# A new hand-written order of the pieces, and four masks placed elsewhere, in a fused threshold-attention and maxout-FFN kernel

## The chip, the core and the metric

The kernel runs on one core of a Trainium2 chip. The metric is the time of one execution in microseconds (us), measured on the device; for a group of runs it is the median. A profile is taken of one execution, and its span goes from the first to the last instruction. The engines are TensorE (PE; its weight loads, PEld, are shown apart), VectorE (DVE), ScalarE (ACT), GpSimd (POOL) and SyncE (SP), which here only issues transfers.

## What is computed

Attention with a threshold: of each row of scaled scores only those within tau = 0.02 of the row's maximum take part in the softmax. Its output, all heads side by side, goes through a maxout network.

```python
# q, k, v: (8, 8, 576, 64) float32; w1, w2, w3: (512, 768); w_out: (768, 512)
scores = scale * np.matmul(q, k.transpose(0, 1, 3, 2))
thresh = np.max(scores, axis=-1, keepdims=True) - tau
scores = np.where(scores >= thresh, scores, -1000000000.0)
scores = scores - np.max(scores, axis=-1, keepdims=True)
attn = np.exp(scores)
attn = attn / (np.sum(attn, axis=-1, keepdims=True) + 1e-09)
attn_out = np.matmul(attn, v)
x = attn_out.transpose(0, 2, 1, 3).reshape(B * S, H * D)      # (4608, 512)
h = np.maximum(np.maximum(x @ w1, x @ w2), x @ w3)
out = h @ w_out
```

## The kernel before

The work is cut into 16 quads (8 batches of two groups of four heads). A quad has 9 chunks of score rows and each chunk two tiles of 128 x 576, so there are 144 chunks and 288 tiles. The last batch is done in two parts of its rows. All scores, transposes, hidden layers, outputs and products pass through four two-bank slots of PSUM, numbered 0 to 3 and called banks below.

A score tile goes like this. PE computes it into a bank (tile `sc`, float32, from `qt`, its half-swapped copy `qs`, and `kt`). DVE takes the row's maximum (`maximum`, line 315). ACT forms what the threshold needs (`exponents`, line 327). Then comes a last pass with the row's sum (`numerators`, line 335). There are two variants, and the string `MASKED` (line 24) chooses one for each tile, with "1" for masked, in the order of the chunks, two digits to a chunk:

- not masked: DVE only reads the bank for the maximum, ACT reads the bank (`exponents`), and ACT makes the last pass as well (`numerators`);
- masked: DVE copies the negated scores to SBUF (tile `z`) together with the maximum, which sets the bank free; ACT works on `z`, and DVE makes the last pass.

Then DVE takes the reciprocals of the chunk's two sums (`reciprocals`, line 341), POOL multiplies both tiles into bfloat16 probabilities `P` (`normalized`, line 345, six buffers), and SP issues a DMA transpose of them into `ptq` (`turned`, line 355). `z` has four buffers for each of the two tiles of a chunk. When a quad's (or part's) chunks are transposed, PE multiplies by `v` (`product`, line 361, tile `o`), DVE and ACT move the result to `xt`, and the FFN (`ffn`, line 434) can run on it: 18 hidden pieces for a batch (tile `ph`; for each block of 128 hidden columns w1, w2 and w3), of which ACT evacuates the first and DVE takes the maximum with the other two, and output pieces (tile `po`), which ACT evacuates and SP stores.

What sets the order is one string, `ORDER` (line 40), read from left to right (lines 718 to 725). Each letter issues one piece (`issue`, line 602), and every engine's instructions are chained in the order in which they are issued (`_Ordered`, line 82). An engine therefore does its own letters in the order of the string; against the other engines it only waits for data and buffers. A digit after S, T, O or F is the bank.

| letter | engine | piece |
|---|---|---|
| S | PE | one score tile |
| T | PE | transposes of q or k for the next quad (tile `tp`) |
| O, N | PE | product of probabilities and v; its ninth rows, for two at once |
| F, B | PE | first and second half of a hidden or output piece |
| m, k | DVE | maximum of a tile; last pass of a masked tile |
| e, n | ACT | exponents of a tile; last pass of a tile that isn't masked |
| r, p, t | DVE, POOL, SP | reciprocals; probabilities (one tile); DMA transpose of a chunk |
| a, c, q | ACT, DVE, POOL | evacuation of transposed q, of transposed k; half-swapped copies `qs` |
| h, v, u | ACT, DVE, ACT | evacuation of the first hidden piece, of the two others, of an output |
| x, w | ACT, DVE | evacuation of a product to `xt` |
| l, y | SP, POOL | loads for a later quad; casts of v |
| g, z | SP, POOL | load of a piece of the weights; its cast to bfloat16 (12 of each) |
| o | SP | store of an output |

"Place" below is the position of a letter (with its digit) in the string, from 0; the string has 2,742. Tiles are numbered from 0 by their digit in `MASKED`. Before the string starts, `beginning` (line 672) transposes the first quad and computes two score tiles.

Of the kernel before, what the change touches and what calls it, by code (L numbers as in the profile page):

```python
# [39 lines left out]
ORDER = """  # L40
mmlS2eS3mmleS1mkllnyT0eS3nS2T1alglermpceS0emT1S3knmaqrpkS1elmqpS2rmeS0ypllneS3mnplleT1mretnnmkS2mcgltlzpqS3e
S0lrpmpeS1etkznenqprnlmpS2S3pmmrmeepS0mnpS2egrpkmpntelS1epmT0kaeerltS3S2tlT0ynmemkeS1nrmpS3ctS2ernnppttT0mlm
pneaS1rtmS3S2pemeS3pqemkmpgneS0rkS1T2qpmqltempyrecpnpS0mqpklS3nemenenS2T1lrpklmerpzapS0pmtryptS3meS2kmeS1S0O
3nnmeempO2NS1eknxrwS0nmeS2rptpqpT3ntmmrnS0tpecmS1pS3eS0tptrmT2S1mmppeatqngleO2ekkleO0rNS3mwxF0elkT2mcnnzpBrp
hS1S2emS0zlpgtpF3F1qemmettkeBqvBS2rnnzF0T3mtBvpnhpkS2meraeF1S0BS3mgevmF2nprS1mepypqBpnF0S3lvkBegF2F1BmhrvS0z
tneBpplzF3nnS2mvBeS1T0mrtT2mhS3pncgpgaS2F0mtBererlmpekvS1emF3S2nntS0pBlemeS1ppzqtS2mvmrF3qentT0pBF1rcmS0pppz
nhenBS3mvO2rmgO1NekglentexnS0F3S1klwmmrnF2plpqypeeBzpBvS0hS1tmF3S2mBtrF1pzpneemrS0vBlneS3mvnS2mrppyS0mnemF1k
S2eS3mreptnepBepmS0F3kpmrS2uutS1kenmnT0arBpekS2emtupueS0mkptpqqO1lltO3emNrlelpkwS2tllxltrlS0F3myF1lmBnpeekph
T2cBF0T3T2vnanqpBS1cvqmF3S2BmneF0hrS1pyperBkF3S2mnBrvmvF0enS1BtS2plmmloppeS3hS0eS1emmtpmF3eekF2BBleF0tlT1vnt
rBvT3aT2haS1pS0kF2crtS3nmBnpmtmF0eS1tqpeeqvBptlmrppF2nveS3lntBmrlF0hS1kpyeBS2mpnvmrenpqyplS3O1qtO0mrNepexkT2  # L50
nS3wF0cS1mrBpmnenS2S1oF3vF0pBtmmeS1pekhlS2toF3rBmmeptynevlT1aBprS2vS0nmmeF1ukketepF3kS1mT2T0rrcBS1ptpqnnaoup
umS0eppmrS2S3mmeeeS0F1eS2qnkpkmT3BS0rnceunrmkmueppS3tlltemO2epO1NotllltS0krwpxS3ppqyF2qnpnmS1BmeS3hF0emmeeF2
BnS1BkrvmnrF3loS0BvpleyyrS2mnpmpphS1ppF0etmS3emllBeF1nF2BtevkrpS0BvS3nS1hmmtleS2lmmetF3tkF0eBpleT1BvrvanT2nF
3cS1BnmF0S2BrhkF3mpeT1vnrBpprveaS0S2nmT1S3pqpncmpS0meeeqmeS1tO2pqmtotlloeO3ltqNF0S1klwBxrpkppS2mrhmF3S0epBmF
2nenS1pvBF0mF3nleBBtottvkS2hF0keF1rurvpmT3BeapkppyrpvS1S2mnS3S0pnemF1mtS3emkS2rpBenepltS0memkmrutpuS2neS3emF
1rmpqkynpS2pqeBemS0uuS2O3kmemekO1NeS0rwT2xoF1olppnT3mnT0BcS2aS3rncqhF0qtF1pBtemmpBkevrF2eS3vlmpnBptnlS0S1S3h
ermmempS2F0ypmF1BBelrteoevnF3T2F0akkqvBBS2nhkymF1pqpnF3verBBS0rvtpmhnS2S1F3mrmlpBpeS0evlmS2eF1pnS3BmnleF2mtl
lvrlttS0eppptyBmS1ehF3lepT2BmltnS0lnltcS1rkvO2O3tmNpmeprT1nnexrapkwS0pqF3qyemT1T2cpBF0S1anepkBS2hvF3S0mreBF1
mekmrnvF2qBeS3vS0unpS2tS1omlrmeppqptlmmnF3pktT0BpecS1eekryuT2uaS0mnS3lomtmrtleF2enpS1kpS3qppnemmS0Bmkerppeue
qS1S0mnurO3kmO1NkwxT0S2eeS1cmpmF3F0kkeBBhF2eF3pvrBS1nnBvpttS0hmemS2mrppF1rpS3BeenmeF0S2vBF1nkvmS3mlnBS0otolh  # L60
F2llterlmF1kBlpypvpBtvteeprS3F0rT2BpS1nnrmpmaS2mtpheS0S3emnF2eT1T0amecBS3ttoS0evyymmS1ppeO2mpqneO3NenqxF0kkt
F1wBT2lolrlklBpS3vphS0cmnF1mtlteS2nqrtBmrpF0vrpqpF3lekBeBpnhF1S2vmT0tlpBS3lS2avmpF0tF1mBrnelekS3evutppmrS2qp
pS1nS0nmF3mrmS1peekenpS2BemmeS0rkS1emuS2tlT0ueT3mcknrannpepF1S0mS3qppBmtotlmlttkrrpeueS0qqmS3lO2ueemoeO0oppt
pkklNwS1lS3xF2mS0BnemehF1kT3mrcnpBS0F2rvS3BltlpnmF1nepmeveS0pkmBS2httnF3eF1mBrBekF0nS2vrBprvpypppS3nmhemeS1S
0F3pF2mmBeBrT1eS0kvnapS3vF1nS2mnBrmmreS3F0pheS1meeBqpnS2mvmeypS1tpS3etlO0qO2mNpmT3neytF1xtlkkrtnweS2ppT0cram
BF3S0BnehvppmeS1rF2qqmT3BF0ncveT3ktnBF2vS1mrnarBhppS0lF3T2qppeBmcS0S1ovmF2mneT3naepBvS0S3enF2mkmrkqpqueenF1n
S2tmS0T3cpqBeupurrS3mmottoS2pS0mttneelotpmS1O3mkkO0rNwrpeexpneF2nkpS0S3S1mBemS0euuppmF1erkS3tltlBptmrF2S0lht
pmeyppBeS1mvO0O3NenmxpS2S1kF0mxemrS3kBF1enF2vBermF0tBhpyppyektBvS1pmF3F2vBkS1BF0nmehS3vrBmtpO2eotpnevO1NkF0S
3krmnrpxpxBhF2S1eBF0mS3F1BnvpmBrS2vS3S0ehemmF1kppmnF2rBvkBF3F0BF1ehBtkvevoF3pptkttO2O0NuprBwS3xS0vmmpeS2ekF1
S3pmF0oeBmrBokettF2peuokoruoF3uhF1pkkF2hvvruF3pF1F2hppF0pvvF3F1vvF2F0F3hvtovhtF1F2F0F3htvF1voF2O0uvO3NvF1xwF  # L70
2hF3F0vF2vhF3F0F2hvF3vvF0F2F3vF0hF2hovF3vF0F2vhF3vvF0vBuuF2BuouoF3uooo
"""


# [684 lines left out]
```

## Time and profile before

| | |
|---|---|
| median of 3 runs | 444.01 us (443.42 to 445.07) |
| the profiled execution | 443.89 us |
| its span | 442.1 us |
| PE busy | 421.6 us (95%) |
| PE weight loads | 306.2 us (69%) |
| DVE busy | 401.2 us (91%) |
| ACT busy | 388.1 us (88%) |
| POOL busy | 320.7 us (73%) |
| granted TensorE clock, mean | 0.988 |

Rows of groups read: line, engine, operation, output from input with shapes, count; busy time and mean length of one in ns; idle time of the engine just before them and what ended most of it. Nearly all instructions carry line 91, the line of the helper that issues them, so the tiles' names tell them apart. Matmuls overlap, and their ends are modelled, so a busy PE isn't PE at its peak. A piece of the chain of waits reads: start, length, engine, tile, line, count.

### The profile page before, as it was taken

The page shows a single profiled execution, that of the slowest core. Times are in us where ns is not written, and L with a number is a line of the kernel's source. Part 1 is how long each engine was busy: PE and PEld are TensorE (multiplying, and loading weights), DVE is VectorE, ACT ScalarE, POOL GpSimd, SP SyncE. Part 2 cuts the span into 40 slices and gives each one's busy share as a digit, 9 for nine tenths or more (in the row PEclk, how much of TensorE's full clock was granted, in tenths as well). Part 3 has the DMA queues.
Part 4 walks back from the last instruction along what each step waited for, and adds up shares of the span by engine and source line. Part 5 has one row for each costly group of instructions (what it writes and reads, how often), then busy time and mean ns, then how long its engine had stood idle before and what let it go on. Part 6 is the DMA issues. An engine that isn't in the chain of part 4 may idle for free.

```text
span 442.1 us, 14065 instructions
## 1 busy us (share of the span) xinstructions
PE 421.6 (95%) x5193; PEld 306.2 (69%) x5193; DVE 401.2 (91%) x1105; ACT 388.1 (88%) x786; POOL 320.7 (73%) x406
## 2 busy tenths in 40 slices
PE   7777799999999999999999999999999999999995
PEld 6443456767778776867687767867677777777762
DVE  2989999999999999999999999999999999999641
ACT  4998999999999999998999999999999999875422
POOL 3898999899976868586777886677769767554500
PEclk9988899999999999999999999999999999999999
DMA  8999989999999998999999999999999978586602
GB/s 234 301 251 204 243 156 223 284 219 213 224 228 177 241 237 169 202 173 283 178 221 188 242 182 222 166 222 193 236 188 177 247 125 165 100 162 137 176 13 108
DMA packets 212773, 87.44 MB, mean 198 GB/s; under 512 B 185824, under 2 KB 199648, under 8 KB 212704
## 3 DMA queue, kind: packets, MB, share of 16 engines
q1 hardware_dynamic: 212000, 85.69, 95.4%
q8 instruction: 41, 0.67, 0.6%
q10 hardware_dynamic: 704, 0.85, 0.6%
q14 instruction: 28, 0.23, 0.2%
HBM read 34.60 MB, written 9.44 MB: 100 GB/s over the span
## 4 chain that ended last, share of the span: by engine, by line
PE 72%; DVE 6%; ACT 4%; POOL 2%; issue 2%; DMA 1%; SPq 0%; POOLq 0%; DVEq 0%
PE ph L91 29%; PE sc L91 25%; PE po L91 9%; PE o L91 6%; ACT z L91 4%; PE tp L91 3%; DVE z L91 2%; DVE unused L91 2%; POOL P L91 1%; POOL qs L91 1%; DVE kt L91 1%; DMA out_dram<-ob 1%; POOL vb L91 0%; DVE xt L91 0%; DVE hT L91 0%
## 5 line engine op out<-in xcount | busy, mean ns | idle before, releaser
L91 POOL TENSOR_SCALAR P<-z,rs 128x576 bf16<-128x576 f32 x288 | 236.2, 834 | 75.2 <-DVE rs L91 21.8
L91 PE MATMUL sc<-kt,qt 64*128 64x320 f32 (+2 forms) x640 | 183.5, 431 | 4.7 <-ACT z L91 2.6
L91 PE MATMUL sc<-kt,qs 64*128 64x256 f32 (+2 forms) x640 | 181.6, 420 | 4.2 <-ACT z L91 2.1
L91 PE MATMUL ph<-xt,w 64*128 64x288 bf16 (+2 forms) x2160 | 170.7, 283 | 0.4 <-DVE xt L91 0.2
L91 PEld LDWEIGHTS <-w 64*128 64x128 bf16 (+1 forms) x2160 | 125.3, 94 | 33.6 <-issue 6.5
L91 DVE TENSOR_SCALAR_CACHE_REDUCE unused<-sc 128x576 bf16<-128x576 f32 x174 | 128.1, 749 | 4.6 <-PE sc L91 3.6
L91 ACT ACTIVATE z<-sc,nm 128x576 f32<-128x576 f32 x174 | 125.3, 740 | 5.3 <-DVE unused L91 2.9
L91 ACT ACTIVATE z<-z 128x576 f32<-128x576 f32 x174 | 117.7, 681 | 0.2
L91 PEld LDWEIGHTS sc<-kt,qs 64*128 64x128 f32 (+1 forms) x640 | 92.2, 179 | 24.3 <-ACT z L91 4.7
L91 PEld LDWEIGHTS sc<-kt,qt 64*128 64x128 f32 (+1 forms) x640 | 91.9, 179 | 19.4 <-ACT z L91 6.2
L91 DVE SCALAR_TENSOR_TENSOR z<-z 128x576 f32<-128x576 f32 x114 | 95.2, 845 | 0.3
L91 ACT ACTIVATE z<-z,nm 128x576 f32<-128x576 f32 x114 | 86.8, 773 | 4.8 <-DVE z L91 4.5
L91 DVE TENSOR_SCALAR_CACHE_REDUCE z<-sc 128x576 f32<-128x576 f32 x114 | 84.7, 751 | 6.9 <-PE sc L91 3.4
L91 POOL COPY qs<-qt 64x640 f32<-64x640 f32 (+3 forms) x68 | 50.2, 738 | 17.8 <-ACT qt L91 14.1
L91 PE MATMUL po<-wo,hT 64*128 64x512 bf16 (+1 forms) x480 | 53.8, 357 | 0.1
L91 ACT ACTIVATE hm<-ph 128x576 bf16<-128x576 f32 (+2 forms) x54 | 32.2, 595 | 20.7 <-PE ph L91 19.8
L91 DVE TENSOR_TENSOR hm<-ph,hm 128x576 bf16<-128x576 f32 (+2 forms) x54 | 37.0, 684 | 8.8 <-PE ph L91 8.7
L91 PEld LDWEIGHTS <-hT 64*128 64x128 bf16 (+1 forms) x480 | 27.5, 97 | 19.0 <-issue 3.8
L91 DVE TENSOR_TENSOR hT<-ph,hm 128x576 bf16<-128x576 f32 (+2 forms) x54 | 37.2, 688 | 2.6 <-PE ph L91 0.5
L91 PE MATMUL o<-ptq,vb 128*64 128x64 bf16 (+2 forms) x544 | 35.3, 281 | 0.1
L91 ACT ACTIVATION_READ_ACCUMULATOR z<-z 128x1 f32 x174 | 34.5, 198 | 0.0
L91 PEld LDWEIGHTS <-vb 128*64 128x64 bf16 x544 | 21.8, 111 | 15.0 <-issue 5.6
(31 smaller groups left out, 257.2 us busy)
## 6 DMA issues: line engine op xcount, KB each, us to landing
vm<-in_v_dram SPq DMA_DIRECT2D x32, 256.0 KB, 5.1
out_dram<-ob SPq DMA_DIRECT2D x31, 256.0 KB, 2.9
qm<-in_q_dram SPq DMA_DIRECT2D x15, 512.0 KB, 4.5
km<-in_k_dram SPq DMA_DIRECT2D x15, 512.0 KB, 5.4
...
ptq<-P SPq DMA_TRANSPOSE x144, 4.1
...
```

The source lines that it names most:

```text
L91: ins = fn(*a, **kw)
```

## The change

Both strings are written anew; all else stays, the number of each letter among it, and 114 tiles are masked in either. In `MASKED` tile 190 passes its mask to 191, and tiles 284 and 285 pass theirs to 277 and 278. In `ORDER` nearly every line differs, since letters stand a few places from where they stood, and the banks of S, T, O and F are assigned anew.

```diff
 MASKED = """
 001110001000100001011000011010010001001000101101001001000000100000011000
 001010100111100001001001000100010001011100101001100010001010010000111000
-110010100101010010011100000001001011000110100110111001000100001110000101
-001010001101110001100001000100100100001100001101010110110101000111111111
+110010100101010010011100000001001011000110100101111001000100001110000101
+001010001101110001100001000100100100001100001101010110110101011111110011
 """
...
 ORDER = """
-mmlS2eS3mmleS1mkllnyT0eS3nS2T1alglermpceS0emT1S3knmaqrpkS1elmqpS2rmeS0ypllneS3mnplleT1mretnnmkS2mcgltlzpqS3e
-S0lrpmpeS1etkznenqprnlmpS2S3pmmrmeepS0mnpS2egrpkmpntelS1epmT0kaeerltS3S2tlT0ynmemkeS1nrmpS3ctS2ernnppttT0mlm
...
-S2eS3mreptnepBepmS0F3kpmrS2uutS1kenmnT0arBpekS2emtupueS0mkptpqqO1lltO3emNrlelpkwS2tllxltrlS0F3myF1lmBnpeekph
...
-3krmnrpxpxBhF2S1eBF0mS3F1BnvpmBrS2vS3S0ehemmF1kppmnF2rBvkBF3F0BF1ehBtkvevoF3pptkttO2O0NuprBwS3xS0vmmpeS2ekF1
-S3pmF0oeBmrBokettF2peuokoruoF3uhF1pkkF2hvvruF3pF1F2hppF0pvvF3F1vvF2F0F3hvtovhtF1F2F0F3htvF1voF2O0uvO3NvF1xwF
-2hF3F0vF2vhF3F0F2hvF3vvF0F2F3vF0hF2hovF3vF0F2vhF3vvF0vBuuF2BuouoF3uooo
+S2S3mlmmeleymS1lT0S3nellglllllmnaS2keerT1mcS0mT1pekmnraelnS3S1pqS2keqmpepyrS3ppmmmneretS0eT1mgknS2menS0letmc
+rS3znqpekmS1pzqlnrmS2prpltmS0plnpeS3peS2lgtnS1mlpmT3enreekmmkS0mprplaeenttS2mkttT3rS1yeS0emnS2pecnrT3nnptmpS
...
+nlS2ekS3mprtpmtkBpeS1S3F2mputrunkS0mtT1elrkBneatpmS3uS0puemO1mpeleO2NpS3qekxS0rppynkwrF1memF2BeT3kBqlchF0vT1
...
+xxeF3krtrppBotS1S2BnhpmF0S1tptrvBF3emS2BmvpemehS1mS0F2F3BF1mekkBF0pvrkBevhteBF2vF1pO3upO0NkBkrS1xwS0vmkmeS3r
+menepF2F1S3nmeBBuF0F3pkrkupuF2huvppF0F1hF3pF0vrvF2pF1hvF3tvphotF0tF2F3vvvF1F0F2htvtoooF3F1ohvF0vO2O3NvwxuF1F
+3hF2F0vF3hvF2vF0F3vhF2vF0F3voF2F0hF3vvF2hF0vF3F2hvF0BuvvuF3BuuooF2ouoo
 """
```

More of the change, by code (lines that the diff above doesn't have):

```diff
@@ L40 @@
 ORDER = """
-mmlS2eS3mmleS1mkllnyT0eS3nS2T1alglermpceS0emT1S3knmaqrpkS1elmqpS2rmeS0ypllneS3mnplleT1mretnnmkS2mcgltlzpqS3e
-S0lrpmpeS1etkznenqprnlmpS2S3pmmrmeepS0mnpS2egrpkmpntelS1epmT0kaeerltS3S2tlT0ynmemkeS1nrmpS3ctS2ernnppttT0mlm
-pneaS1rtmS3S2pemeS3pqemkmpgneS0rkS1T2qpmqltempyrecpnpS0mqpklS3nemenenS2T1lrpklmerpzapS0pmtryptS3meS2kmeS1S0O
-3nnmeempO2NS1eknxrwS0nmeS2rptpqpT3ntmmrnS0tpecmS1pS3eS0tptrmT2S1mmppeatqngleO2ekkleO0rNS3mwxF0elkT2mcnnzpBrp
-hS1S2emS0zlpgtpF3F1qemmettkeBqvBS2rnnzF0T3mtBvpnhpkS2meraeF1S0BS3mgevmF2nprS1mepypqBpnF0S3lvkBegF2F1BmhrvS0z
@@ L46 @@
-tneBpplzF3nnS2mvBeS1T0mrtT2mhS3pncgpgaS2F0mtBererlmpekvS1emF3S2nntS0pBlemeS1ppzqtS2mvmrF3qentT0pBF1rcmS0pppz
-nhenBS3mvO2rmgO1NekglentexnS0F3S1klwmmrnF2plpqypeeBzpBvS0hS1tmF3S2mBtrF1pzpneemrS0vBlneS3mvnS2mrppyS0mnemF1k
-S2eS3mreptnepBepmS0F3kpmrS2uutS1kenmnT0arBpekS2emtupueS0mkptpqqO1lltO3emNrlelpkwS2tllxltrlS0F3myF1lmBnpeekph
-T2cBF0T3T2vnanqpBS1cvqmF3S2BmneF0hrS1pyperBkF3S2mnBrvmvF0enS1BtS2plmmloppeS3hS0eS1emmtpmF3eekF2BBleF0tlT1vnt
-rBvT3aT2haS1pS0kF2crtS3nmBnpmtmF0eS1tqpeeqvBptlmrppF2nveS3lntBmrlF0hS1kpyeBS2mpnvmrenpqyplS3O1qtO0mrNepexkT2
@@ L51 @@
[L51 to L65, printed above, removed]
@@ L66 @@
-BF3S0BnehvppmeS1rF2qqmT3BF0ncveT3ktnBF2vS1mrnarBhppS0lF3T2qppeBmcS0S1ovmF2mneT3naepBvS0S3enF2mkmrkqpqueenF1n
-S2tmS0T3cpqBeupurrS3mmottoS2pS0mttneelotpmS1O3mkkO0rNwrpeexpneF2nkpS0S3S1mBemS0euuppmF1erkS3tltlBptmrF2S0lht
-pmeyppBeS1mvO0O3NenmxpS2S1kF0mxemrS3kBF1enF2vBermF0tBhpyppyektBvS1pmF3F2vBkS1BF0nmehS3vrBmtpO2eotpnevO1NkF0S
-3krmnrpxpxBhF2S1eBF0mS3F1BnvpmBrS2vS3S0ehemmF1kppmnF2rBvkBF3F0BF1ehBtkvevoF3pptkttO2O0NuprBwS3xS0vmmpeS2ekF1
-S3pmF0oeBmrBokettF2peuokoruoF3uhF1pkkF2hvvruF3pF1F2hppF0pvvF3F1vvF2F0F3hvtovhtF1F2F0F3htvF1voF2O0uvO3NvF1xwF
@@ L71 @@
-2hF3F0vF2vhF3F0F2hvF3vvF0F2F3vF0hF2hovF3vF0F2vhF3vvF0vBuuF2BuouoF3uooo
+S2S3mlmmeleymS1lT0S3nellglllllmnaS2keerT1mcS0mT1pekmnraelnS3S1pqS2keqmpepyrS3ppmmmneretS0eT1mgknS2menS0letmc
+rS3znqpekmS1pzqlnrmS2prpltmS0plnpeS3peS2lgtnS1mlpmT3enreekmmkS0mprplaeenttS2mkttT3rS1yeS0emnS2pecnrT3nnptmpS
+1S0emrpS2pampmlemS0ekmrqS3peS1knqepT2temqS3gpyS0nlprtlnpmcpS2eqemekS1mlrptkT3nmeS0ltnpzarmeS2ttpeprS3mepnyS1
+kO0mneO2memrNkppeS3pwnS1xmrmnprptS2mT0eneS1tpS3cS0mmnptrtT1eqpmS2gllmaeeneS3pleqO1kO2NkrS0mlwmkzT1pcxF2eS3tn
@@ new lines @@
+reBpnhmeS0S1mzF2F3epBmgBeS0kvpF1T2trnqqmvBS0nntF3tkhS1arBmgS2pmevmrpyzeF0ppS3BeF1mnlvekS2BF0gntrerF3mqBhpplt
+S1neBnnvF2meS0BvS3pzpmhT1T0rznaS2empeS0cmmgppF1eBgekrS3nvtF2S0mnS1elBmppeqzS3mtpevrmnS0F2lpT1cnBntF3heqztS1B
+rmS0mvmrpgO2pO3keenleNkwS1xgS0F3nmF2BtlrmnpqpeBrvlS1metpS0phF3S2nypzenBmrmF0ptvS1pzppeByeS3mS2vnmrmneS1eemF0
+nlS2ekS3mprtpmtkBpeS1S3F2mputrunkS0mtT1elrkBneatpmS3uS0puemO1mpeleO2NpS3qekxS0rppynkwrF1memF2BeT3kBqlchF0vT1
+T3naBS2npcF1qS3vqmBpyF0mrrltlneklS2mhppetBnF1S3reltlpvmBnvF0eS2pBhrmS3meS1myeS0mS2eF1pmlF3epBeBF0kvpnvT2Blat
@@ new lines @@
+lT1hT3kqS2S0ancnF3pmS1eqBmrrmeF0vS2lpltlettBtlmvtptnenqpF3pqS1BmhellrkF0S2tnmBS3vnyppS1mmreprO2O0eNeT3S1kpxF
+0lnwocnS2meBrpmS3S2F1vF0mpBnemepS2rkmS3heBtpF1mnT2vBS3prveaS0enmpF2ypoeympktkF1ueS3lkmT2rT0nnBcaeppqtrrS3otu
+mtotS0S2pummS1eS0epqmekkpenF3S2mprT1BS0lcmlltnrS1euO2munkpO3eempNkrS0ewS1xpmF2mS3BnS1qnehpF0tmeltmkretlF2npq
+pBltlolepnS3vBrmevppypF0lS1BomthneS2S3F1S0mrmBmF3peF2neBvS1krBeS0nhvmpmS3S2mF0eempF1peeBT3kBtT2avrF0tnS3vcnm
+rBnF1kS2ptmhlopBpeF0tT3nlBevrtrllqaS1S2vT3S0mcqnpppS1pmlnS3mqmmeekO2O0eNwreeF1kS3mqxBpypS2rF0tnhmpS1BmypeF3S
@@ new lines @@
+2lplveemoklBF1F0BtnotkrvpelhnnBF2S1vmF3upkrepT0BS3pvltaS1rtnpmS0F2S3memrenkS0memS1teepBumS3S1kmrS0pqpuF2mS1e
+pBmpktenenS3eumS1kO0uerrmppmkppyO2NweeS3mxT1F2T0ncrnqpT3aeBhtlnpS1S0comlqF3F2mlBeBqeknF1S0vrvprmBnhepS3S2yS0
+mS1F3mmoF2ltemppBeeveBkF0rkT1F3BavS1BnottlF2qhmF0nnpBpBtrvyotlttlS3enlS1thkvlpyS2mrpppmmrF0eeeBvS3S1mF2nS0pB
+nmeeF1rmvS3pmeBpS2F0hmenlqltntT1pencBkrtS3S2ppvO1mmO0rnNkT2exS3wF0ppaT1meT2BaqcF3krS1vmBnehqS2rF0pS3mkyoBltl
+emF1pvrqpeeF2nupBS0vS3mS2mnmtppS1F0T3emBkS1rqecnelT2eulkryS3uamS0F2mppnmrS0tettpS1eeltpkmpnlmS3BmkqpS1reenpS
@@ new lines @@
+0qemO3O1pueruNkxT2mktwcS0mkS1tlltelpnF3F2BemkpBhrvF0rpeF3BS1BS2vpnpmS0mnhpmlF1ereS3BF2etlS0mpnevkBF1nmS3vBnh
+emS0rF2F1BrmkvBvepotteS3F0ntT2nBypprpapmrhS1meS2S0eS3mmltF2pypT1mT0peqnaBS3ecevmpeS0tqnS1O2O3NmemF0keF1Blkqx
+wT3BnS2nrkrpvcS0htmnpmF1S3BqprmyF0eF2eBepvrkovpBnF1S3lllhnT0pBS2mapvqS3oF0lempF1BmeketurS2vS3S1mprtlnpS0nmlm
+ptlF2eS1motlletetprneS3kompemeBrkS0S1ppuqmmS3utT0tT2cpltF1S0eknaS2nermmpeBnpkmS0lS3O2eurmpO0euerpmqekolltNxp
+pkwnS1mS3mrkF2S0lepemBtlhqF1pnT3BS2F0ennrcvS3BF1mepS2BmvrkmeS0pmF3hF1BBkneF2eS0vrnBnS3vS1mhptlS2pyyptmopetme
@@ new lines @@
+F3F0mrptkptreBteBvT1vS2mnanS3F1S0nBmppmS3ermqF2hprpS1eBemeS0evS1mpltnS3mO2pllqmeO0neNtkkrxwT3F1S0enT2BcaF3S2
+BmvpyS1nqpremmF0qpheT3BcF2T3BvneF0S1BakrnrpqpnphvltqS3ppmrF2peT0nmBcvS3S1F0T2mepBlttttonmtS3atooveenS2mqF0yr
+F1ppqmeueS3S0kknmT2BnecrpmS2rpS3mpmS0uuepmkneeS1oO2rmnO0NxepwkekF3prS0nmeS2S1BmppeS0mukrumF1pyS2BehpetttS3F0
+S1BmmtrpO3emvnpO2eNoS1koxxmS0F3F2eBemltkBrpvltS0F1ehmkF3nnBBrS2ppevmF0S1vtBomkF2etF3phnBeyrpS0BpvO1mvO2kNF0k
+xxeF3krtrppBotS1S2BnhpmF0S1tptrvBF3emS2BmvpemehS1mS0F2F3BF1mekkBF0pvrkBevhteBF2vF1pO3upO0NkBkrS1xwS0vmkmeS3r
```

## The prediction

> **What bounds the kernel now.** I read busy time by stretches first, then the chain of waits for the price of unhindered work on TensorE (PE), and counted PE's work against the clock. The columns are busy time (and instructions) of PE, PE's weight loads, DVE, ACT and POOL, then granted clock, DMA share, GB/s.
>
> ```profile
> core 0: us, PE busy (x) PEld busy (x) DVE busy (x) ACT busy (x) POOL busy (x), PEclk, DMA share, GB/s
> 20.00:40.00 20.00, 14.19 (x100) 8.54 (x104) 18.39 (x54) 18.75 (x42) 17.98 (x23) 0.83 1.14 231
> 40.00:60.00 20.00, 16.48 (x150) 9.92 (x146) 18.79 (x59) 19.77 (x42) 19.21 (x24) 0.91 1.03 219
> 60.00:80.00 20.00, 18.96 (x235) 13.50 (x229) 19.51 (x54) 19.35 (x41) 18.98 (x23) 1.00 0.96 224
> 80.00:100.00 20.00, 19.77 (x262) 14.21 (x260) 18.79 (x51) 19.78 (x42) 18.44 (x22) 1.00 1.10 245
> ...
> 380.00:420.00 40.00, 40.00 (x526) 31.38 (x524) 34.82 (x93) 24.16 (x48) 21.33 (x24) 1.00 0.65 139
> ...
> 0.00:100.00 100.00, 84.67 (x875) 56.55 (x877) 87.71 (x244) 91.43 (x189) 85.60 (x111) 0.95 1.03 236
> 100.00:435.00 335.00, 334.38 (x4298) 248.54 (x4293) 313.05 (x861) 295.40 (x596) 235.07 (x295) 1.00 0.96 187
> ```
>
> There are two regimes. Up to 100 us PE has gaps and the three softmax engines are full: from 20 to 100 us ACT is idle 80 - (18.75+19.77+19.35+19.78) = 2.35 us, DVE 4.5, POOL 5.4. From 100 us to 435 PE is never idle by its busy time. As the ends of matmuls are modelled, that alone proves little, so I price unhindered work. These are pieces of the chain of waits and two lines of the timeline (start, length, what):
>
> ```profile
> 195.00 2.47 PE o L91 x40
> ...
> 207.31 2.00 PE sc L91 x16
> ...
> 216.38 1.29 PE po L91 x12
> ...
> 224.85 2.46 PE ph L91 x40
> ...
> 411.20 7.97 PE ph L91 x72
> ...
> 422.73 9.89 PE ph L91 x72
> ...
> 205.52 0.84 PE L91 MATMUL po<-wo,hT 128*64 128x256 bf16 x12
> 206.30 0.52 PE L91 MATMUL tp<-identf,qm 64*128 64x64 f32 x10
> 206.66 0.65 PE L91 MATMUL ph<-xt,w 64*128 64x288 bf16 x8
> ```
>
> A score tile (4 matmuls, sc) costs 2.00/4 = 0.50 us, a wide hidden matmul 2.46/40 = 0.0615, an output matmul 1.29/12 = 0.1075 (narrow 0.07), a product matmul 2.47/40 = 0.062, a transpose (206.66-206.30)/10 = 0.036. The counts from 100 us on, by tile, are rows of the stretches for sc, ph, po, o and tp in that order, and the two odd forms:
>
> ```profile
> 100.00:438.00 338.00, 136.88 (x958) 1.00 0.96 187
> 100.00:438.00 338.00, 151.78 (x1928) 1.00 0.96 187
> 100.00:438.00 338.00, 53.84 (x480) 1.00 0.96 187
> 100.00:438.00 338.00, 33.82 (x560) 1.00 0.96 187
> 100.00:438.00 338.00, 20.09 (x396) 1.00 0.96 187
> ...
> L91 PE MATMUL sc<-kt,qt 64*64 64x320 f32 x96 | 14.1, 442 | 0.0
> ...
> L91 PE MATMUL po<-wo,hT 128*64 128x256 bf16 x96 | 6.8, 277 | 0.0
> ```
>
> Of the 958, 192 (twice 96) are the 64-column form, 8 to a tile; so tiles are 766/4 + 192/8 = 215.5, or 107.8 us. Hidden: 1784 x 0.0615 + 7.97 + 9.89 = 127.6. Output: 384 x 0.1075 + 96 x 0.07 = 48.0. Products 34.6, transposes 14.3. Together 332.3 us of the 337.6 up to PE's last matmul. From 100 us on PE is the bound, and an order can win back at most 5.3 us there; before that, at most ACT's 2.35.
>
> The Trainium skill, "Perfetto Trace Analysis", section "Identifying the Most-Contended Engine", says that matmul busy time doesn't tell how near PE is to its limit and that the busy share of weight loads should be read beside the work done per peak. By that rule PE would have a quarter left from 100 us on (248.54/335 = 74%), DVE would be the bound, and an order would have more to win; the count above speaks against it, and the rule's case is the second rival.
>
> **The change part by part.** Both texts have the same letters, 2,742 of them, and 114 masked tiles: nothing is added or removed.
>
> *Masks.* Tile 190 hands its mask to 191, and 284 and 285 hand theirs to 277 and 278. A masked tile costs DVE an extra pass and spares ACT one of similar length. The two, and a weight cast on POOL, are rows of the page's groups (count, busy us, mean ns, idle before):
>
> ```profile
> L91 DVE SCALAR_TENSOR_TENSOR z<-z 128x576 f32<-128x576 f32 x114 | 95.2, 845 | 0.3
> ...
> L91 ACT ACTIVATE z<-z 128x576 f32<-128x576 f32 x174 | 117.7, 681 | 0.2
> ...
> L91 POOL CAST w<-stage 128x1024 bf16<-128x1024 f32 x9 | 10.3, 1145 | 0.2
> ```
>
> So two passes of some 0.8 us come earlier on DVE, from behind the last scores to before them; ACT gives and gets the same two. The swap at 190 is nil.
>
> *Order.* The score letters stand 4 places from where they stood in the median and 18 at most, hidden pieces and readers alike; 100 places take some 14.5 us (place 101 is reached at 24.5 us, 2,700 at 425.4), so that is 0.6 us and up to 2.6. I weighed every letter by its start-to-start time without a wait, for instance 0.67 us for a maximum on DVE:
>
> ```profile
> 208.03 0.75 DVE L91 TENSOR_SCALAR_CACHE_REDUCE z<-sc 128x576 f32<-128x576 f32 x1
> 208.70 0.08 DVE L91 DVE_READ_ACCUMULATOR z<-sc 128x1 f32 x1
> 208.70 0.75 DVE L91 TENSOR_SCALAR_CACHE_REDUCE unused<-sc 128x576 bf16<-128x576 f32 x1
> ```
>
> and compared what the engines have done at equal ACT work. Between 20 and 350 us of it PE and DVE stand within 0.2 us of the old order in every stretch but the first (PE 0.6 ahead between 20 and 40, where it has gaps anyway). The new order doesn't bring PE's work forward. POOL differs: between 60 and 100 us of ACT's work it has 1.0 us less to do, since weight casts (z, 1.1 us each) go back from places 398, 455, 463, 590, 607 to 424, 472, 479, 602, 615. POOL is 95% busy there, so probabilities reach their products up to 1.0 us sooner, or not at all sooner where ACT decides. ACT and POOL are both nearly full: I take the middle, **-0.5** (0 to -1.0). The casts still precede their first use; the tightest, at 424, is 24 places (3.5 us) ahead of the hidden piece at 448 that reads it, where it was 50. Its 1.1 us fits; if POOL came 2.4 us late there, that piece would hold PE.
>
> *PE's waits in the first regime.* One goes, at 23.4 us:
>
> ```profile
> 23.39 0.90 PE L91 MATMUL sc<-kt,qt 64*128 64x320 f32 x1 [0.72 <-ACT z L91]
> ```
>
> The score at place 91 took the bank that the ACT letter just ahead of it (90) was reading; the new one, at 92, takes a bank read at 75, 1.5 us earlier. But ACT was full meanwhile, so I cost it at nothing, between nothing and the 0.7 us of the wait. PE's other waits of this kind stay: their piece still follows the last reader of its bank.
>
> *Bank hand-overs in the second regime.* To see where the new order is late, I put each of its letters at the time at which its engine had done the same amount of work in the profiled execution. Of 566 pieces of PE, 13 between 100 and 390 us would find their bank late, by 4.3 us in sum, none over 0.6; the old order has 2 by this reading. What PE loses now in that stretch is of the same size (5.3). One redraw for another: I take **-0.9**, a sixth of the 5.3, with -5.3 and +4.3 as ends.
>
> *Ahead of the last scores.* DVE has 2.2 us more to do before the last score tile than it had (the two passes, and one more maximum, 2 x 0.75 + 0.67), and 2.8 less behind it. DVE is 34.82/40 busy from 380 us on, so most of it goes into gaps; the last score tile's bank is read by a maximum that would come 1.1 us late by the same laying out. I take half, **+0.5** (0 to +1.1).
>
> *SyncE's queue.* Transposes, loads and stores move by up to 149 places against the rest, but it is their place in the queue that counts. The queue stands mostly behind POOL:
>
> ```profile
> SPq L91 <- POOL P L91: 119.4, 95, 3.2
> ...
> ptq<-P SPq DMA_TRANSPOSE x144, 4.1
> ...
> L91 POOL TENSOR_SCALAR P<-z,rs 128x576 bf16<-128x576 f32 x222 | 181.8, 832 | 69.6 <-issue 20.8 <-DVE rs L91 18.7 <-ACT z L91 14.0
> ```
>
> A transpose stuck behind a load or store that isn't ready is rarer in the new text (16 held over 2 us, not 18), and by the same laying out a probability buffer is written again no sooner than 2.7 us after its transpose should have landed in the old text and 5.5 in the new (landing 4.1 us after the issue). Nothing. If that cover went, POOL would wait, and it has 69.6 us idle before such products from 100 us on.
>
> *The end.* After the last products both texts give PE the same work; and the pieces that end the chain are the same:
>
> ```profile
> 419.94 1.39 PE o L91 x40
> 421.33 1.40 PE po L91 x12
> 422.73 9.89 PE ph L91 x72
> 432.61 2.59 PE po L91 x23
> ...
> 435.39 2.29 DMA out_dram<-ob
> 437.68 0.41 DVE obr L91
> ```
>
> Nothing, either way.
>
> **The sum.** The profiled execution took 443.89 us (span 442.1 and 1.8 around it), 0.1 under the median of the runs. 443.89 - 0.5 - 0.9 + 0.5 = **443.0 us**. Its own range is 441.8 to 446.1, within 0.5%, which is about what a measurement of this kernel can tell from no change.
>
> **The rivals.** *The leftover is really won.* Half of ACT's 2.35 us and half of PE's 5.3: 443.9 - 1.2 - 2.6 = **440.1**. For it: all the waits are small collisions of 0.2 to 1.5 us, the kind that moves of 2 us can undo. Against it: equal progress of PE at equal ACT work.
>
> *DVE is the bound* from 100 us on. DVE idles 335 - 313.05 = 22 us there; an order that wins a third gives 443.9 - 7.3 = **436.6**. For it: DVE's 93%. Against it: PE's counted 332.3 of 337.6, which no order of DVE shortens. (The rule of the Trainium skill quoted above would put it so.)
>
> *New late hand-overs hit PE directly.* The late pieces come to 1.0 us before 100, 4.3 up to 390 and 5.9 after it (11 pieces around 396 to 413 us, up to 1.1 each). Where PE has no slack each is lost, unless one delay covers the next. Half of 11.2: 443.9 + 5.6 - 0.5 = **449.0**; all of it 454.6, a third 447.1. It decides from some 2.7 us of net loss on. For it: PE is full, and waits of score loads on ACT and DVE are already there. Against it: delays overlap, and the old order's own 5.3 go.
>
> *The order does nothing*, as each engine follows the others within a few pieces: 443.9, inside the forecast's own range.
>
> **How the numbers follow.** Forecast (with the last case) 0.45, leftover won 0.23, DVE the bound 0.08, late hand-overs 0.24. The range 438.5 to 448.5 leaves out the DVE case, a little of the first and the worse third of the third: under 0.2. Faster 0.23 + 0.08 + 0.01 of the forecast's edge = 0.32; slower 0.24 + 0.01 = 0.25; same 0.43.
>
> **What would show it.** Right: PE's counted work from 100 us on again 332, the end 4 to 7 us above it; POOL's casts later with ACT's busy time in the first 100 us as before or up to 1 us more; the stretch from the last products to the end 20.8 us (442.1 - 421.3). The wait at 23.4 us gone, without the end moving. Wrong: PE's busy time under 334 in 335 us after the first 100, or PE more than 1 us ahead or behind in matmuls done at 100 us; waits of score loads in the stretch 395 to 410 us would speak for the late hand-overs.

## The result, and the profile after

| | median us | runs | profiled execution | span |
|---|---|---|---|---|
| before | 444.29 (443.38 to 445.07) | 7 | 443.89 | 442.1 |
| after | 445.68 (445.14 to 446.71) | 7 | 445.86 | 444.1 |

The ratio is 1.0038, with a 95% interval of 1.0022 to 1.0054: slower by 1.4 us, where 443.0 was forecast. The time lies in the range and in the forecast's own range, but the sign is wrong.

The stretches of the new kernel, with the columns of the prediction's first fence:

```profile
0.00:100.00 100.00, 83.03 (x865) 55.69 (x867) 87.63 (x243) 90.69 (x187) 83.89 (x111) 0.97 1.07 233
100.00:435.00 335.00, 334.25 (x4286) 247.88 (x4284) 313.43 (x862) 295.94 (x596) 229.62 (x296) 1.00 0.94 188
60.00:80.00 20.00, 18.24 (x234) 13.76 (x228) 19.46 (x53) 19.18 (x40) 18.92 (x23) 1.00 1.06 219
80.00:100.00 20.00, 19.52 (x254) 13.57 (x251) 19.26 (x50) 19.14 (x42) 16.97 (x22) 1.00 1.15 241
380.00:420.00 40.00, 40.00 (x531) 31.44 (x528) 34.95 (x95) 25.52 (x51) 17.63 (x24) 1.00 0.60 118
```

Busy shares hardly differ: PE 334.25 of 335 us after the first 100, and 334.38 before. Such a table can't show where 2 us of span went. Pieces that stand in both chains of waits can. The end of the new one:

```profile
404.12 1.39 PE o L91 x40
406.10 1.51 PE sc L91 x12
...
413.22 7.97 PE ph L91 x72
424.75 9.89 PE ph L91 x72
```

Before, the same four pieces start at 402.09, 404.08, 411.20 and 422.73 (the last two stand in the prediction):

```profile
402.09 1.39 PE o L91 x40
404.08 1.51 PE sc L91 x12
```

The new kernel is 2.02 to 2.03 us behind at each. All of it was lost before 404 us, and the last scores and the tail lose nothing. The medians differ by less, by 1.4 us, since the old kernel's profiled execution lies 0.4 us under its median and the new one's 0.2 us over. To find where the 2 us were lost, I laid both traces over each other by DVE's work: when does each kernel start the instruction that stands behind the same sum of DVE work, each instruction weighed by the median length of its kind? These are computed lags behind the old kernel's profile, in us, each a mean over a stretch (a minus means ahead); the other kernels are the experiments below:

```
kernel               60-80  120-140  300-320  340-360  420-438
after                 0.07     1.25     1.19     1.97     2.02
x_casts_moved         0.16     1.17     1.11     1.19     1.26
x_after_then_before   0.28     1.18     2.62     2.59     2.60
x_before_then_after  -0.24    -0.20     0.53     1.33     1.40
x_poolbefore         -0.14     0.83     1.97     3.10     3.43
x_oneinput_before    -3.20    -3.29    -3.67    -3.78    -3.04
x_oneinput_after     -2.29    -2.14    -2.26    -2.31    -1.60
x_six_long            0.01    -0.58    -0.65     0.14     0.26
x_six_short           1.13     1.35     1.29     2.09     2.22
x_cast_onto_pass     -0.31    -0.39    -0.43    -0.03    -0.03
x_first_cast         -0.80    -0.56    -0.57    -0.58    -0.58
x_masks_only          1.80     1.79     2.04     2.03     3.42
x_three_casts        -0.33     0.71     0.70     0.77     0.83
```

Three of these kernels issue exactly the old order in their first 200 us, and they stand at -0.24, -0.31 and +1.80 at 60 to 80 us: the first stretch scatters by that much from one execution to the next, and its lags say little. From there to 200 us the same three stay flat within 0.1. So steps behind 80 us can be read, and the new kernel has two: 1.2 us between 80 and 130 us, and 0.8 us at 332 us. Nothing else adds to it. The two x_oneinput rows drift, since 114 of their DVE instructions are others: by TensorE's last hidden pieces, which start at 417.98 and 419.42 us instead of 422.73, those kernels end 4.75 and 3.31 us ahead. One of the 12 runs of x_six_short took 1059.8 us and is left out of its median below.

At the second step one instruction stands out. The timeline of the new kernel there, DVE first and then POOL:

```profile
331.92 0.75 DVE L91 TENSOR_SCALAR_CACHE_REDUCE unused<-sc 128x576 bf16<-128x576 f32 x1
332.59 0.08 DVE L91 DVE_READ_ACCUMULATOR unused<-sc 128x1 f32 x1
332.59 1.65 DVE L91 SCALAR_TENSOR_TENSOR z<-z 128x576 f32<-128x576 f32 x1
...
330.75 1.89 POOL L91 TENSOR_SCALAR P<-z,rs 128x576 bf16<-128x576 f32 x2 [0.66 <-DVE rs L91]
332.59 1.03 POOL L91 CAST vb<-vm 128x1024 bf16<-128x1024 f32 x1
333.57 0.82 POOL L91 CAST vrb<-vr 128x128 bf16<-128x128 f32 x1
```

The masked last pass (`SCALAR_TENSOR_TENSOR`, letter k) takes 1.65 us and starts together with a value cast of 1.03 us on POOL. The small cast behind it takes 0.82 us. In the old kernel the same pass and that cast don't meet:

```profile
331.43 0.74 DVE L91 SCALAR_TENSOR_TENSOR z<-z 128x576 f32<-128x576 f32 x1
...
333.45 1.03 POOL L91 CAST vb<-vm 128x1024 bf16<-128x1024 f32 x1
...
340.91 0.29 POOL L91 CAST vrb<-vr 128x128 bf16<-128x128 f32 x1
```

So the pass takes 0.74 us by itself, and 1.65 us behind a cast that it meets: it waits until the cast is done, and the next instruction of POOL then waits for the pass (0.82 us where it takes 0.29). The maximum, which reads the scores from PSUM, takes 0.73 to 0.76 us in all 288 tiles of this trace, whatever POOL does. The pass is given `zn` twice from SBUF (`in0=zn, in1=zn`), and that is what sets it apart. I call it theory P: a pass and an instruction of POOL exclude each other, the one that starts first goes through, and a new order changes which of them meet.

The Trainium skill, "SBUF — State Buffer", section "Who interferes with whom", states such a rule: a DVE instruction with two SBUF inputs and a GpSimd instruction that reads SBUF contend for a pair of ports that they share, the pair is an exclusive lock, and the order of issue decides which of the two blocks. The rows above agree (1.65 us in place of 0.74, and 0.82 in place of 0.29); the prediction didn't weigh it.

The first step has six such passes. The groups of the stretch from 79.5 to 130 us, first before, then after:

```profile
L91 DVE SCALAR_TENSOR_TENSOR z<-z 128x576 f32<-128x576 f32 x12 | 10.5, 881 | 0.0
```

```profile
L91 DVE SCALAR_TENSOR_TENSOR z<-z 128x576 f32<-128x576 f32 x12 | 11.8, 988 | 0.0
```

Twelve passes take 1.3 us more. In the new kernel those at 80.2, 88.4, 98.4, 109.4, 115.0 and 122.4 us take 1.13 to 1.30 us; in the old one only two, at 114.0 and 117.9 us, take 1.20 and 1.26. In the trace each of the six starts 0.02 to 0.58 us after a probability tile or a copy has started on POOL. And TensorE feels it. Waits from 80 to 130 us, before and after (engine, for what, us in all, times, longest):

```profile
PEld sc L91 <- ACT z L91: 1.4, 5, 0.5
PEld sc L91 <- DVE z L91: 0.4, 1, 0.4
```

```profile
PEld sc L91 <- ACT z L91: 1.7, 5, 0.5
PEld sc L91 <- DVE z L91: 1.7, 3, 0.7
```

Score loads wait 1.3 us more for a bank that DVE still has to read; I put that down to maxima that stand behind a long pass on DVE. In x_six_long below, where the six passes are short, this wait is 0.4 us again.

Over the whole kernel the excess is the same in both, since the mean pass takes 845 ns before and 849 after. What the new order changed is where it falls: onto stretches in which DVE has no slack and TensorE waits for it.

### The profile page after: what moved, and what is told of

Its sections match the earlier page's. It is cut to its first block, busy times and chain, and to the rows that moved or that the text cites. A ratio compares the mean times of both kernels' runs of the same rounds, so it can differ in the third digit from the quotient of the medians.

```text
span 444.1 us, 14062 instructions
## 1 busy us (share of the span) xinstructions
PE 421.9 (95%) x5193; PEld 305.5 (69%) x5193; DVE 401.8 (90%) x1105; ACT 388.8 (88%) x786; POOL 313.5 (71%) x406
## 4 chain that ended last, share of the span: by engine, by line
PE 69%; DVE 16%; issue 7%; ACT 5%; DMA 1%; POOL 1%; DVEq 0%; ACTq 0%; POOLq 0%
PE ph L91 27%; PE sc L91 24%; PE po L91 8%; DVE z L91 8%; PE o L91 7%; DVE unused L91 5%; ACT z L91 4%; PE tp L91 3%; DMA qm<-in_q_dram 1%; DVE hT L91 1%; DVE kt L91 1%; DVE rs L91 1%; DVE xt L91 0%; DVE hm L91 0%; POOL P L91 0%
## 5 line engine op out<-in xcount | busy, mean ns | idle before, releaser
L91 POOL TENSOR_SCALAR P<-z,rs 128x576 bf16<-128x576 f32 x288 | 228.2, 805 | 82.6 <-DVE rs L91 39.9
L91 PEld LDWEIGHTS sc<-kt,qs 64*128 64x128 f32 (+1 forms) x640 | 91.2, 177 | 25.4 <-ACT z L91 6.3
L91 PEld LDWEIGHTS sc<-kt,qt 64*128 64x128 f32 (+1 forms) x640 | 90.7, 177 | 22.2 <-ACT z L91 6.5
L91 PEld LDWEIGHTS <-hT 64*128 64x128 bf16 (+1 forms) x480 | 28.4, 97 | 18.3 <-issue 3.8
```

The costliest lines, as they stand in the source:

```text
L91: ins = fn(*a, **kw)
```

## The experiments

"Subtractions" in the expectations are POOL's P letters, which multiply a tile by its reciprocals. The old kernel ran beside each batch, with medians of 444.31 to 444.50 us.

| run | median us | ratio to before | 95% interval |
|---|---|---|---|
| x_casts_moved | 445.22 | 1.0015 | 1.0003 to 1.0027 |
| x_after_then_before | 446.52 | 1.0050 | 1.0035 to 1.0064 |
| x_before_then_after | 445.57 | 1.0032 | 1.0019 to 1.0046 |
| x_poolbefore | 447.68 | 1.0075 | 1.0059 to 1.0090 |
| x_oneinput_before | 439.04 | 0.9882 | 0.9861 to 0.9903 |
| x_oneinput_after | 440.38 | 0.9892 | 0.9871 to 0.9914 |
| x_six_long | 444.22 | 1.0000 | 0.9986 to 1.0014 |
| x_six_short | 445.38 | 1.0021 | 1.0007 to 1.0035 |
| x_cast_onto_pass | 444.13 | 1.0000 | 0.9986 to 1.0014 |
| x_first_cast | 443.27 | 0.9980 | 0.9966 to 0.9994 |
| x_masks_only | 445.88 | 1.0034 | 1.0019 to 1.0049 |
| x_three_casts | 444.91 | 1.0010 | 1.0001 to 1.0019 |

**The casts at 332 us, moved away** (x_casts_moved), in the new kernel:

```diff
-...S1mhptlS2pyyptmopetme
+...S1mhptlS2pptmopyyetme
```

> The new kernel with one change: the two value casts on POOL that start at 332.6 us (yy of ORDER line 64) stand two subtractions later in POOL's order. Theory P (a masked pass k on VectorE reads two inputs from SBUF and shares its way there with POOL, so that it takes 1.65 us instead of 0.75 us beside the value cast of 1.03 us): that k falls below 1.1 us and the end comes 0.5 to 0.8 us earlier, 445.0 against 445.7 us, unless the casts meet another k further on, which the trace would show as a k over 1.2 us behind 333 us. Rival (the new order of TensorE hands its banks over late there, whatever POOL does): no change, 445.5 to 445.9 us.

The same place in its timeline:

```profile
332.53 0.75 DVE L91 SCALAR_TENSOR_TENSOR z<-z 128x576 f32<-128x576 f32 x1
...
334.19 1.47 POOL L91 TENSOR_SCALAR P<-z,rs 128x576 bf16<-128x576 f32 x2 [1.61 <-ACT z L91]
335.60 1.04 POOL L91 CAST vb<-vm 128x1024 bf16<-128x1024 f32 x1
```

The pass takes 0.75 us, the step is gone from the lag (1.11 at 300 us, 1.19 at 340), and the median falls by 0.46 us, just under the 0.5 to 0.8 expected. The intervals of the two ratios overlap, so the median alone doesn't prove the gain; the step in the lag does. The order of every other engine is untouched, so this step was the meeting of cast and pass.

**One half of each order** (x_after_then_before, x_before_then_after): all engines take one order up to place 1280, at about 203 us, and the other from there, with the masks of the second order.

```diff
 ORDER = """
-(places 0 to 1279 of the one text)(places from 1280 of the same text)
+(places 0 to 1279 of the one text)(all letters still to come, in the order of the other text)
```

> The new order of all engines up to place 1280 of the written order (about 203 us), from there on the old order. Theory P (the loss is made where long masked passes fall into stretches in which VectorE has no slack: 1.2 us between 80 and 130 us, 0.8 us at 332 us): the first part of the loss is kept, the second is gone, about 1.0 to 1.3 us over the old kernel, 445.3 to 445.6 us. Rival (the loss comes from late hand-overs in the second half of the new order or from its tail): level with the old kernel, 444.0 to 444.5 us.

> The old order of all engines up to place 1280 of the written order (about 203 us), from there on the new order. Theory P: only the loss at 332 us is made, 0.6 to 0.9 us over the old kernel, about 445.0 us, and the trace shows the masked pass of 1.65 us beside the value cast again. Rival (the loss is all in the first half): level with the old kernel; rival (it is all in the second half): 445.7 us as the new kernel.

Both missed: the first is 0.9 us above theory P's 445.3 to 445.6, the second 0.6 above its 445.0. The lags say why: the seam itself costs 1.5 us between 200 and 230 us in the one and 0.7 in the other. Apart from the seam the parts are where they were expected, 1.18 us at 130 us in the first, and a second step of 0.80 (0.53 to 1.33) in the second. The medians alone would have settled nothing.

**The old order on POOL alone** (x_poolbefore): the letters p, q, y and z of the new text in the old sequence.

```diff
 ORDER = """
-(the new text)
+(the new text, its letters p, q, y, z among themselves in the sequence of the old text)
```

> The new kernel with the old order of POOL's instructions (subtractions, exponent sums, casts), all other engines in the new order. Theory P: a masked pass is long where POOL's work falls on it, so another POOL order moves the long passes; the sum of all masked passes stays near 11 us over 0.75 us each, and the end moves by up to 1.5 us either way with the places of the long passes; after 100 us the lag steps only where a masked pass is over 1.1 us. Rival (the new order of POOL is itself late, by its weight and value casts, without the masked passes): back to 444.3 us. Rival (the loss is in TensorE's order): stays at 445.7 us.

447.68 us, 2.0 above the new kernel. So two rivals fall: that POOL's new order is late by itself (444.3 us), and that TensorE's order alone sets the time (445.7 us). The excursion is larger than the 1.5 us of the expectation; the passes are longer (their mean is 860 ns, 849 in the new kernel), and the lag grows in steps up to 400 us. Which meetings make each step was not followed up.

**The exclusion taken away everywhere** (x_oneinput_before, x_oneinput_after): the pass as an operation with one SBUF input. This leaves out the zeroing of masked values; they become the threshold.

```diff
-            vector.scalar_tensor_tensor(out=zn, in0=zn, scalar=thr, in1=zn,
-                                        op0=OP.is_ge, op1=OP.mult, accum_out=acc)
+            vector.tensor_scalar(out=zn, in0=zn, scalar1=thr, scalar2=None,
+                                 op0=OP.max, op1=OP.add, accum_out=acc)
```

> The old kernel with the masked pass of the numerators as an operation with a single input from SBUF (the larger of value and threshold, summed, in place of the product of the comparison and the value): masked values below the threshold become the threshold instead of zero, nothing else changes. Theory P (two inputs from SBUF exclude POOL's instructions): no pass is over 0.85 us beside POOL's work, POOL's subtractions fall to 0.75 us each beside it, the 11 us over 0.75 us in all passes vanish, and the kernel is 1 to 4 us faster, most of it before 100 us. Rival (long passes come from something else, as a late operand or the write): passes beside POOL's work stay at 0.85 to 1.28 us and the time stays near 444.3 us.

> The new kernel with the same exchange: the masked pass as an operation with a single input from SBUF, masked values below the threshold become the threshold. Theory P: without the exclusion the collisions at 80 to 130 us and at 332 us cost nothing, and the new order stands within 0.5 us of the old order with the same exchange. Rival (the loss lies in bank hand-overs, casts or the tail of the new order): it stays 1.2 to 1.6 us behind the old order with the same exchange.

Groups of the old kernel, as it was and with the exchange:

```profile
L91 POOL TENSOR_SCALAR P<-z,rs 128x576 bf16<-128x576 f32 x288 | 236.2, 834 | 75.2 <-DVE rs L91 21.8
...
L91 DVE SCALAR_TENSOR_TENSOR z<-z 128x576 f32<-128x576 f32 x114 | 95.2, 845 | 0.3
```

```profile
L91 POOL TENSOR_SCALAR P<-z,rs 128x576 bf16<-128x576 f32 x288 | 210.7, 744 | 101.8 <-DVE rs L91 36.8
...
L91 DVE TENSOR_SCALAR_CACHE_REDUCE z<-z 128x576 f32<-128x576 f32 x114 | 83.6, 744 | 1.4 <-ACT z L91 1.0
```

Every pass now takes its 0.74 us, and POOL's products fall from 834 to 744 ns, 288 x 0.09 = 26 us of POOL's time. The kernel is 1.2% faster, 5.5 us by the medians (444.50 to 439.04), more than the 1 to 4 expected; by the lags 3.2 us of it are there at 60 to 80 us already. So the mechanism is shown, on both engines, and its price.

The second half of the expectation missed: with the exchange the new order still stands 1.3 us behind the old one by the medians (440.38 and 439.04), which is the rival's figure. That difference is not sure: the intervals of the ratios, 0.9871 to 0.9914 and 0.9861 to 0.9903, overlap, and two of the six runs (438.65 and 438.85 us) are level with the old order's. In the traces the loss has another place. The wait of TensorE at 62 us in the new order with the exchange:

```profile
61.95 2.14 PE L91 MATMUL o<-ptq,vb 128*64 128x512 bf16 x31 [0.70 <-DMA ptq<-P]
```

Running 2 to 3 us earlier, the order asks for products before their probabilities are transposed. An order fits one set of durations, and this kernel had others. The difference of the two rows of lags is 0.91 us at 60 to 80 us already, 1.15 at 120 to 140, 1.41 at 300 to 320 and 1.47 at 340 to 360. So without the exclusion the two steps of 1.2 and 0.8 us shrink to 0.24 and 0.06, as theory P has it. As most of the difference lies in the stretch that scatters, a smaller cut was needed all the same.

**Only the six long passes, and six others as a control** (x_six_long, x_six_short), in the new kernel. In the six tiles the masked values become the threshold.

```diff
-        if masked(g, idx, r):
+        if (number[g, idx], r) in ((26, 1), (30, 0), (34, 0), (37, 0), (40, 1), (42, 0)):
+            vector.tensor_scalar(out=zn, in0=zn, scalar1=thr, scalar2=None,
+                                 op0=OP.max, op1=OP.add, accum_out=acc)
+        elif masked(g, idx, r):
```

The control has (33, 1), (38, 0), (39, 0), (41, 0), (41, 1), (44, 1) in their place.

> The new kernel with six masked passes alone exchanged for the operation with one input from SBUF, the six that took 1.13 to 1.30 us between 80 and 130 us (masked values below the threshold become the threshold in these six tiles). Theory P (the first 1.2 us are lost in these six passes, which hold POOL off or are held off by it): each takes 0.75 us, the lag of 1.2 us at 130 us falls to 0.4 us or less, and the end comes 0.8 to 1.4 us earlier, 444.3 to 444.9 us. Rival (that stretch loses by its order: operands and banks that come late, whatever the passes take): the passes are short and the end stays at 445.3 to 445.9 us.

> Control: the same exchange in the six other masked passes of the same stretch of the new kernel, those that took 0.73 to 0.86 us between 97 and 128 us. Theory P: no change but for one pass of 0.86 us and run to run scatter, 445.4 to 445.9 us. If this one gains as much as the exchange in the long passes, theory P is wrong about the place.

The six long ones exchanged bring 1.46 us (445.68 to 444.22), a little more than expected, and the kernel is level with the old one; the lag at 130 us goes from +1.25 to -0.58. The six others bring 0.30 us, which the intervals don't tell from nothing. Long against short, the intervals of the two ratios still touch (up to 1.0014 and from 1.0007). One of the long passes, in the new kernel and with the exchange, with what POOL does meanwhile:

```profile
122.39 1.30 DVE L91 SCALAR_TENSOR_TENSOR z<-z 128x576 f32<-128x576 f32 x1
...
121.28 1.03 POOL L91 CAST vb<-vm 128x1024 bf16<-128x1024 f32 x1
122.37 0.71 POOL L91 COPY qs<-qt 64x640 f32<-64x640 f32 x1
```

```profile
120.77 0.75 DVE L91 TENSOR_SCALAR_CACHE_REDUCE z<-z 128x576 f32<-128x576 f32 x1
...
119.80 1.03 POOL L91 CAST vb<-vm 128x1024 bf16<-128x1024 f32 x1
120.89 0.71 POOL L91 COPY qs<-qt 64x640 f32<-64x640 f32 x1
```

The long pass starts 0.02 us after the copy: the copy's rest of 0.69 and 0.75, less 0.13, makes 1.31. In the second trace the copy runs beside the exchanged pass, and both keep their length. The control isn't clean: with other passes short, the six long ones fell from 7.3 us in sum to 6.1 in its profile, and its lag, high from the start (1.13), grows by only 0.22 up to 130 us, where that of the new kernel grows by 1.18. The step goes with the long passes there too, but that six other passes leave it as it was is told by the medians alone.

**A meeting made in the old kernel** (x_cast_onto_pass):

```diff
-...nepmeveS0pkmBS2httnF3eF1mBrBekF0nS2vrBprvypppp...
+...nepmeveS0pykmBS2httnF3eF1mBrBekF0nS2vrBprvpppp...
```

> The old kernel with one letter moved: the value cast on POOL that starts at 333.45 us stands four subtractions earlier, where POOL waits (329.0 us), so that it meets the masked pass of 329.32 us on VectorE. Theory P: that pass takes 1.4 to 1.65 us instead of 0.75 us, and the end comes 0.5 to 0.8 us later, 444.9 to 445.2 us against 444.4 us. Rival (VectorE has slack there, the loss of the new kernel at 332 us was its order): no change.

```profile
328.90 1.28 DVE L91 SCALAR_TENSOR_TENSOR z<-z 128x576 f32<-128x576 f32 x1
...
328.53 1.04 POOL L91 CAST vb<-vm 128x1024 bf16<-128x1024 f32 x1
```

The edit moves the cast past two of POOL's tiles, not four as the expectation says. The pass met the cast 0.37 us after its start, and took 1.28 us, 0.53 more than by itself and less than the 1.4 to 1.65 expected. The lag steps from -0.43 to -0.03 there and stays: 0.40 us, somewhat under the 0.5 to 0.8 expected. The medians show no change, with an interval of 0.6 us either way, so this cost is read from the trace alone.

**The first long pass avoided in the old kernel** (x_first_cast). Both kernels have a pass of 1.65 us beside a value cast at 33 us. In the old one:

```profile
33.17 1.65 DVE L91 SCALAR_TENSOR_TENSOR z<-z 128x576 f32<-128x576 f32 x1
...
33.17 1.03 POOL L91 CAST vb<-vm 128x1024 bf16<-128x1024 f32 x1
```

```diff
-...S3S2tlT0ynmemkeS1nrmpS3ctS2ernnppttT0mlm
+...S3S2tlT0nmemkeS1nrmpS3ctS2ernnpypttT0mlm
```

> The old kernel with one letter moved: the value cast on POOL that starts at 33.17 us together with a masked pass of 1.65 us stands two subtractions later. Theory P: that pass falls below 1.1 us, and as ACT, VectorE and POOL are all full there, the stretch to 60 us runs 0.4 to 0.9 us earlier and the end comes 0.3 to 0.9 us earlier, 443.5 to 444.1 us, provided that the subtractions behind the cast are not late. Rival (the stretch is set by ACT, or the cast is in the way of the subtractions just as much in its new place): no change, or up to 0.5 us later.

```profile
32.78 0.75 DVE L91 SCALAR_TENSOR_TENSOR z<-z 128x576 f32<-128x576 f32 x1
...
34.87 0.96 DVE L91 SCALAR_TENSOR_TENSOR z<-z 128x576 f32<-128x576 f32 x1
...
35.18 1.55 POOL L91 CAST vb<-vm 128x1024 bf16<-128x1024 f32 x1
```

Now the cast comes second, waits for the pass at 34.87 us (1.55 us in place of 1.03), and DVE goes on. The median is 443.27 us, 0.2 below the range expected, and a ratio of 0.9980 (0.9966 to 0.9994): one letter moved gives a kernel that beats both, if only by 0.2%. The lags can't place the gain, as it lies in the stretch that scatters. Part of the gain is given back at 74.0 us, where a pass of 0.75 us in the old profile takes 1.22.

**The new masks alone** (x_masks_only): the old order, with k and n exchanged for the six tiles and one half of a hidden piece (F0) two letters later, behind its bank's reader.

```diff
 MASKED = """
-...00110111001000100001110000101  (tile 190)   ...101000111111111  (tiles 276 to 287)
+...00101111001000100001110000101               ...101011111110011
```

> The old kernel with the new MASKED string alone: the old order, with the last passes of six tiles changed between VectorE and ACT where the masks need it. All six tiles lie behind 255 us. Theory P (the loss lies in the six long passes between 80 and 130 us and in the cast at 332 us): no part of it is the masks', 444.0 to 444.6 us. Rival (the four moved masks take a part): 444.8 us or more.

A miss: 445.88 us. The lag rises by 1.4 us between 400 and 410 us. Its chain of waits there:

```profile
399.66 2.12 DVE z L91 x7
...
404.89 1.68 PE o L91 x36
407.17 1.51 PE sc L91 x12
```

The last scores, after TensorE has waited 0.26 us for `hT` on DVE, start 3.09 us behind those of the old kernel (404.08), though its lag was 2.0 until 400 us: two passes that used to lie behind the last scores now lie ahead of them, and the chain goes through DVE. The moved F0 lies in the same stretch, and no run separates its share. The new order has the same masks and pays nothing there (2.02 to 2.03 at each piece from 404 us on). So masks and order belong together, and the loss of the whole change isn't the masks'.

**Three casts moved in the new kernel** (x_three_casts): those of x_casts_moved and of x_first_cast.

```diff
-...ttT3rS1yeS0emnS2pecnrT3nnptmpS
+...ttT3rS1eS0emnS2pecnrT3nnpytmpS
...
-...S1mhptlS2pyyptmopetme
+...S1mhptlS2pptmopyeytme
```

> The new kernel with three value casts moved on POOL: the two at 332.6 us, as before, and the one at 32.8 us, which stands two subtractions later, as in the run that did this to the old kernel. Theory P: both passes of 1.65 us fall below 1.1 us; what the cast at 332.6 us cost (0.5 us in the medians) and what the cast at 33 us cost in the old kernel (1.0 us) come off, 444.0 to 444.8 us, if the six long passes between 80 and 130 us stay as they are. Rival (phase decides, and a shift of 0.9 us ahead of 80 us draws the long passes between 80 and 130 us anew): anywhere between 443.3 and 446.0 us, with other passes long in that stretch.

444.91 us, 0.1 above theory P's range. By its lag to the new kernel it is 1.2 us ahead at 40 to 60 us and only 0.4 at 60 to 80: at 51.6 us another pass now takes 1.54 us, behind a weight cast. The rival's redraw between 80 and 130 us didn't come: that stretch has 11.7 us of masked passes, as in the new kernel (11.8). But passes were drawn anew ahead of it, and so the price of one meeting can't be summed blindly with that of the next. How much of that is scatter, one profile doesn't tell.

## Why the prediction was right or wrong

**The bound.** Right: after 100 us the new kernel's PE has the same work, 958 score matmuls and 1,936 hidden ones (8 more than before), so 332.3 + 8 x 0.0615 = 332.8 us, of the 339.7 up to its last matmul (437.40 + 2.26). What PE loses there rose from 5.3 to 6.9 us.

**"One redraw for another: I take -0.9".** This is the step that failed: the bank hand-overs in the second regime, and the way in which they were priced. It laid the letters out "by its start-to-start time without a wait", one time for each, and priced the masked pass "some 0.8 us" from the group's mean. But a mean of 845 ns hides passes of 0.74 to 1.65 us, and which are long is drawn by the order itself, through POOL. The laying out couldn't see the meetings. The value casts (y), one of which makes the meeting at 332 us, stand up to 141 places from where they stood, and no term weighed them. The runs put +1.46 us (x_six_long) on the six passes from 80 to 130 us and +0.46 (x_casts_moved; 0.8 by the lag) on the one at 332 us, where the term had -0.9. Three of the six, at 80.2, 88.4 and 98.4 us, lie before 100 us, so a part of the +1.46 stands against the term of -0.5 below, which was worked out with the same single lengths. The sum, 1.9, is more than the 1.4 us lost; that both undone at once would give it all was not tried.

**The signs named.** None of those for being wrong shows: PE is busy 334.25 of 335 us, where under 334 was to be the sign, and at 100 us it stands 10 matmuls behind (865 and 875), some 0.8 us at the 262 in 20 us of the old kernel. Busy time and counts were too coarse for a loss of this size. One sum of the prediction is off: (425.4 - 24.5)/2,599 x 100 makes 15.4 us for 100 places, not 14.5. Nothing hangs on it.

**"I take the middle, -0.5", POOL's relief before 100 us.** The casts did move back: POOL's busy time from 60 to 100 us fell from 37.42 to 35.89 us. But POOL only waited more for reciprocals (39.9 us in the whole kernel, 21.8 before), and at 60 to 80 us the new kernel is level (0.07); behind 80 us the first step begins. The first 80 us scatter between executions by more than this term, so nothing shows a gain there. That x_oneinput_before is 3.2 us ahead at 60 to 80 us suggests that this stretch does reward shorter passes.

**"I take half, +0.5", ahead of the last scores.** The mechanism is real, as the new masks in the old order lose 1.4 us there (with the moved F0), but the new order has made room, and the term is 0 for the whole change. The swap at 190 wasn't quite nil in the old order: the pass of that tile lies at about 270 us, and the lag of x_masks_only goes from 1.79 at 120 to 140 us to 2.04 at 300 to 320. In the new order no such step shows (1.25 and 1.19).

**The wait at 23.4 us** is gone without a gain; another one of 1.46 us, for reciprocals, stands at 24.31 us. **SyncE's queue** shows no loss, as no third step stands in the lag. **The end** holds: 444.1 - 423.35 = 20.75 us behind the last products (421.96 + 1.39), and 20.8 were forecast.

**The rivals.** New late hand-overs at 396 to 413 us fall, as the lag is flat there. Between 80 and 130 us score loads do wait longer for their banks, as that rival had it, but x_six_long shows that it was the passes' length and not the order of the hand-overs. The leftover wasn't won. That DVE is the bound falls as stated: DVE is 313.43 of 335 us busy, as before, and the kernel is slower. But DVE's lengths do set part of TensorE's leftover: x_oneinput_before gains 5.5 us, some 1.5 of them behind 80 us (3.2 ahead there, 4.75 at the end).
